# A Strassen-type output product, with two groups laced, for the last three tiles of a retention and bilinear-FFN kernel

## The chip, the cores and the metric

The kernel runs on one core of one Trainium2 chip. The metric is the device time of one launch in microseconds; the lower the better. Engines are named as in the profile: PE (TensorE, the matmuls), PEld (its weight loads), DVE (VectorE), ACT (ScalarE), POOL (GpSimd), SP (SyncE, which here only issues DMAs).

## The reference

Four batches of eight heads, 768 positions and head size 64 go through a recurrent retention, and its output, 3072 tokens of 512 values, through a bilinear feed-forward layer. All inputs and the output are float32.

```
gamma = 1.0 - 2.0 ** (-5.0 - arange(H))
for t in range(S):
    state = gamma * state + einsum('bhd,bhe->bhde', k[:, :, t], v[:, :, t])
    y[:, :, t] = scale * einsum('bhd,bhde->bhe', q[:, :, t], state)
x = y.transpose(0, 2, 1, 3).reshape(3072, 512)
a = x @ w_a          # 512 x 1536
b = x @ w_b          # 512 x 1536
out = (a * b) @ w_out  # 1536 x 512
```

## The kernel before

The tokens lie in 24 slots of 128. The feed-forward layer takes them in eight tiles `J` of 4, 2, 2, 2, 2, 4, 4 and 4 slots (`TILES`). The retention works in chunks of one slot: `casts(t)` scales k and q by powers of gamma on GpSimd, casts v, and has a DMA transpose k and q; `turn(new, old)` issues the scores of two new slots with their masks on VectorE (`scores`), the updates of the state, and the outputs of two old slots (`inter`, `intra`, `leave`), which become columns of the tile's `xt`. The first six slots go through `casts2`, `scores2` and their like, which work on pairs.

A block `ft` of the layer (`ffn_ab`, 12 blocks in a tile) computes 128 of the 1536 hidden values for all tokens of the tile: four matmuls into `a`, an ACT copy of it into `asb` (bf16), four matmuls into `g`, and on VectorE the product of `g` (in PSUM) and `asb` into `ht[J][:, ft]` (line 445). After the blocks, `ffn_out(J, i)` multiplies row `i` of the tile (128 tokens): 12 matmuls, one for each `ft`, with `ht` as weights and 512 columns of `wo_bf` streaming, accumulated in one PSUM bank `o`, copied by ACT into `osb` and stored. The last row of the last tile is cut into 256, 128 and 128 columns, the middle one copied by VectorE.

Every engine's order is the program's order: `seq` ties each instruction to the one before it on its engine. The order of the work is written out by hand at the end of the function: blocks, turns, casts and output rows of different tiles stand between one another, so that TensorE has work while others wait. What runs in tiles 5 to 7 before the change:

```
    blocks(5, 6, 9)
    turn(20, 18)
    blocks(5, 9, NFT)
    outs(5, 0, 1, 2, 3)
    blocks(6, 0, 4)
    turn(22, 20)
    blocks(6, 4, 9)
    turn(None, 22)
    blocks(6, 9, NFT)
    outs(6, 0, 1, 2, 3)
    blocks(7, 0, NFT)
    outs(7, 0, 1, 2, 3)
```

PSUM has eight banks: a ring of three for `a`, `g`, `o` and some scores (tag "ff"), one each for `y0` and `y1`, a pair for `at`, one for the state. Weights arrive in float32 slices in the pool `wstage` (four buffers each for two tags, 4 KB a partition), issued by SyncE in the order of `LOADS`, and are cast by GpSimd (`cast_w`, `cast_o`) into `wa_bf`, `wb_bf` and `wo_bf`. Each load waits for the cast that frees its buffer; the loads behind it in SyncE's queue wait with it. Stores of tiles 0 to 4 are held until the next block and issued by SyncE, those of tiles 5 to 7 by ACT.

Of the kernel before, what the change touches and what calls it, by code (L numbers as in the profile page):

```python
# [9 lines left out]
F32 = mybir.dt.float32  # L10
BF16 = mybir.dt.bfloat16
AF = mybir.ActivationFunctionType
ALU = mybir.AluOpType


TILES = [4, 2, 2, 2, 2, 4, 4, 4]
# [7 lines left out]
def kernel(  # L24
# [10 lines left out]
    nc = tc.nc  # L35
    P = 128
    B, H, S, D = q.shape
    NCH = S // P
    HP = H // 2
    DM = H * D  # L40
    DFF = moe_w_a.shape[1]
    KT = DM // P
    NFT = DFF // P
    NSLOT = B * NCH
    NW = 6
    WC = DFF // NW
    FPW = NFT // NW
    NO = 6
    FPO = NFT // NO
# [3 lines left out]

    const = ctx.enter_context(tc.tile_pool(name="const", bufs=1))
    wpool = ctx.enter_context(tc.tile_pool(name="wpool", bufs=1))
    wstage = ctx.enter_context(tc.tile_pool(name="wstage", bufs=4))
    raw = ctx.enter_context(tc.tile_pool(name="raw", bufs=3))
    nat = ctx.enter_context(tc.tile_pool(name="nat", bufs=6))
    tra = ctx.enter_context(tc.tile_pool(name="tra", bufs=4))
# [3 lines left out]
    osbp = ctx.enter_context(tc.tile_pool(name="osbp", bufs=6))  # L63
    psff = ctx.enter_context(tc.tile_pool(name="psff", bufs=3, space=bass.MemoryType.PSUM))
    psat = ctx.enter_context(tc.tile_pool(name="psat", bufs=1, space=bass.MemoryType.PSUM))
# [6 lines left out]
    def seq(bi):  # L72
        ins = bi.ins
        prev = last.get(ins.engine)
        if prev is not None:
            tc.add_manual_dep(ins, prev.name, nosync, reason="program order")
        last[ins.engine] = ins
        return bi


    raws, wst, whole = {}, {}, {}
# [17 lines left out]

    def load_w(j):  # L100
        for nm, src in (("a", moe_w_a), ("b", moe_w_b)):
            st = wstage.tile([P, KT, WC], F32, tag="w" + nm, name="wst" + nm)
            s = src[:, j * WC : (j + 1) * WC].rearrange("(c p) f -> p c f", p=P)
            seq(nc.sync.dma_start(out=st, in_=s))
            wst[nm, j] = st

    def load_o(j):
        st = wstage.tile([P, FPO, DM], F32, tag="w" + "ab"[j % 2], name="wsto")
        s = moe_w_out[j * FPO * P : (j + 1) * FPO * P, :].rearrange("(c p) d -> p c d", p=P)
        seq(nc.sync.dma_start(out=st, in_=s))  # L110
        wst["o", j] = st
# [3 lines left out]
    def issue_loads(n):  # L115
        for _ in range(min(n, len(pending))):
            what = pending.pop(0)
            {"p": load_pair, "s": load_slot, "w": load_w, "o": load_o}[what[0]](int(what[1:]))
# [2 lines left out]
    kqb = {}  # L121
    kqb = {}
    issue_loads(6)
    zero = const.tile([P, HP * P], F32, name="zero")
    seq(nc.vector.memset(zero, 0.0))  # L125
    lgr = const.tile([P, 1, H], F32, name="lgr")
    bq = const.tile([P, 1], F32, name="bq")
# [26 lines left out]
    for par in range(2):  # L154
        m = const.tile([P, 1, P], BF16, name=f"mask{par}")
# [17 lines left out]
    wa_bf = wpool.tile([P, KT, DFF], BF16, name="wa_bf")  # L173
    wb_bf = wpool.tile([P, KT, DFF], BF16, name="wb_bf")
    wo_bf = wpool.tile([P, NFT, DM], BF16, name="wo_bf")

    def cast(engine, dst, src):
        if engine is nc.scalar:
            seq(nc.scalar.copy(dst, src))  # L179
        else:  # L180
            seq(engine.tensor_copy(dst, src))  # L181
# [13 lines left out]
    first = 0  # L195
# [36 lines left out]
    def half(i):  # L232
        return slice(64 * i, 64 * i + 64)

    def scores(t, ff):
        if ff:
            at = [psff.tile([P, HP, P], F32, tag="ff", name=f"at{r}") for r in range(2)]
        else:
            both = psat.tile([P, 2, HP, P], F32, tag="at", name="at")
            at = [both[:, r] for r in range(2)]  # L240
        for hp in range(HP):
            for c in range(2):
                for r in range(2):
                    seq(nc.tensor.matmul(at[r][half(c), hp, :], kqT[t][half(r), 0, hp, half(c)],  # L244
                                         kqT[t][half(r), 1, hp, :], start=True, stop=True,
                                         skip_group_check=True))
        aT[t] = tra.tile([P, 2, HP, P], BF16, tag="aT", name="aT")
        for r in range(2):
            seq(nc.vector.tensor_tensor(aT[t][:, r], at[r], mask.to_broadcast([P, HP, P]), op=ALU.mult))  # L249
# [43 lines left out]
    def leave(t):  # L293
        J, i = where[t]
        if i == 0:
            xt[J] = xtp.tile([P, KT, 4 * P], BF16, tag="xt", name="xt")
        for r in range(2):
            seq(nc.scalar.copy(  # L298
                xt[J][:, 2 * r : 2 * r + 2, i * P : (i + 2) * P].rearrange(
                    "p j (s n) -> p j s n", s=2),  # L300
                ys[t // 2][r].rearrange("p (s j) n -> p j s n", s=2)))
# [23 lines left out]
    kqT2 = {}  # L325
# [19 lines left out]
    def scores2(u, par, ff=False):  # L345
        t = 2 * u + par
        if not ff:
            both = psat.tile([P, 2, HP, P], F32, tag="at", name="at")
            at = [both[:, r] for r in range(2)]
        else:  # L350
            at = [psff.tile([P, HP, P], F32, tag="ff", name=f"at{r}") for r in range(2)]
        for hp in range(HP):
            for c in range(2):
                for r in range(2):
                    seq(nc.tensor.matmul(at[r][half(c), hp, :],  # L355
                                         kqT2[u][half(r), par, 0, hp, half(c)],
                                         kqT2[u][half(r), :, 1, hp, half(c)],
                                         start=True, stop=True, skip_group_check=True))
        aT[t] = tra.tile([P, 2, HP, P], BF16, tag="aT", name="aT")
        for r in range(2):  # L360
            seq(nc.vector.tensor_tensor(aT[t][:, r], at[r], masks[par].to_broadcast([P, HP, P]),  # L361
                                        op=ALU.mult))
# [48 lines left out]
    def xcols(J, kt, c0, c1):  # L411
        if J < 2:
            return xt[J][:, c0 // P : c1 // P, kt, :]
        return xt[J][:, kt, c0:c1]
# [7 lines left out]
    ht = {}  # L422

    asbs = {}
# [13 lines left out]
    def ffn_g(J, ft, c0=0, c1=None):  # L438
        c1 = TILES[J] * P if c1 is None else c1
        fs = slice(ft * P, (ft + 1) * P)  # L440
        g = psff.tile([P, 4 * P], F32, tag="ff", name="g")[:, : c1 - c0]
        for kt in range(KT):
            seq(nc.tensor.matmul(g, wb_bf[:, kt, fs], xcols(J, kt, c0, c1),  # L443
                                 start=(kt == 0), stop=(kt == KT - 1)))
        seq(nc.vector.tensor_tensor(ht[J][:, ft, c0:c1], g, asbs.pop((J, ft, c0)), op=ALU.mult))  # L445

    def ffn_ab(J, ft):
        store()
        ffn_a(J, ft)
        ffn_g(J, ft)  # L450

    held = []

    def store():
        for dst, src in held:
            seq(nc.sync.dma_start(out=dst, in_=src))
        held.clear()

    def ffn_out(J, i):
        store()  # L460
        n0 = (sum(TILES[:J]) + i) * P
        osb = osbp.tile([P, DM], F32, tag="osb", name="osb")
        ends = J == len(TILES) - 1 and i == TILES[J] - 1
        cols = [(0, DM // 2), (DM // 2, 3 * DM // 4), (3 * DM // 4, DM)] if ends else [(0, DM)]
        for c0, c1 in cols:
            o = psff.tile([P, DM], F32, tag="ff", name="o")[:, : c1 - c0]
            for ft in range(NFT):
                seq(nc.tensor.matmul(o, ht[J][:, ft, i * P : (i + 1) * P], wo_bf[:, ft, c0:c1],  # L468
                                     start=(ft == 0), stop=(ft == NFT - 1)))
            cast(nc.vector if c0 == DM // 2 else nc.scalar, osb[:, c0:c1], o)  # L470
            if c0 == DM // 2:
                continue
            b0 = DM // 2 if c0 else 0
            dst, src = out[n0 : n0 + P, b0:c1], osb[:, b0:c1]
            if J < 5:
                held.append((dst, src))
            else:
                seq((nc.sync if c0 else nc.scalar).dma_start(out=dst, in_=src))

    D_, G_, A_ = nc.vector, nc.gpsimd, nc.scalar  # L480
    K, Q = 0, 1
# [5 lines left out]
    flip2(0, Q, [((0,), D_)])  # L487
    warm(psat, "y1", 256)
    scores2(0, 1)
    scores2(0, 0, True)  # L490
    update2(0, 0)
    warm(psat, "y1", 512)
# [60 lines left out]
    def blocks(J, a, b):  # L553
        for ft in range(a, b):
            ffn_ab(J, ft)

    def outs(J, *rows):
        for i in rows:
            ffn_out(J, i)

    casts(6)
    blocks(1, 0, 3)
    casts(7)
    blocks(1, 3, NFT)
    outs(0, 0, 1)
    casts(8)
    outs(0, 2, 3)
    casts(9)
# [42 lines left out]
    blocks(5, 6, 9)  # L611
    turn(20, 18)
    blocks(5, 9, NFT)
    outs(5, 0, 1, 2, 3)
    blocks(6, 0, 4)
    turn(22, 20)
    blocks(6, 4, 9)
    turn(None, 22)
    blocks(6, 9, NFT)
    outs(6, 0, 1, 2, 3)  # L620
    blocks(7, 0, NFT)
    outs(7, 0, 1, 2, 3)


# [28 lines left out]
```

## Time and profile before

| | |
|---|---|
| time, median of 3 runs | 231.83 us (231.5 to 232.21) |
| span of the profiled execution | 229.7 us, 5165 instructions |
| granted TensorE clock, mean | 0.998 |
| PE busy | 223.5 us (97%), 2108 matmuls |
| DVE, ACT, POOL busy | 95.1, 85.5, 77.0 us (41, 37, 34%) |
| output product, matmuls of 512 columns | 276 |
| HBM read, written | 28.31 MB, 6.29 MB |

The span runs from the first to the last instruction of one profiled execution; its own time as a launch is not given apart from the runs, whose times also contain what lies around the span. Times in the traces count from the span's start. In the groups of instructions the columns are: line, engine, operation, written tile <- read tiles, shapes, count, then busy microseconds and mean nanoseconds of one, then the engine's idle time before them and what ended it. In the chain the columns are start, microseconds, and what. In the timeline they are start, microseconds, engine, line and operation.

### The profile page before, as it was taken

To read this page: it belongs to the slowest core of one execution; us is meant where nothing else is said; L and a number is where in the kernel's file an instruction comes from. 1 tells how busy PE (TensorE), PEld (TensorE's weight loads), DVE (VectorE), ACT (ScalarE), POOL (GpSimd) and SP (SyncE) were. 2 spreads that over 40 slices of the span, in tenths; PEclk is the share of its full clock that TensorE was granted. 3 is DMA by queue.
4 is the path that set the end of the run, shared out by engine and by line. 5 is a ranking of instruction groups with operands and counts; after the bars stand their busy time and mean duration, and the time that the engine had idled before them with its cause. 6 is when DMAs were issued, how large, how long until landed. Compare 5 with 4: busy or idle time off the path is not lost.

```text
span 229.7 us, 5165 instructions
## 1 busy us (share of the span) xinstructions
PE 223.5 (97%) x2108; PEld 130.2 (57%) x2108; DVE 95.1 (41%) x178; ACT 85.5 (37%) x176; POOL 77.0 (34%) x98
## 2 busy tenths in 40 slices
PE   7899999999999999999999999999999999999994
PEld 3567445686456866887685454544454444444443
DVE  3785348542041565463644264620264310243300
ACT  3364334342225334454443453622343422433222
POOL 5355776776634254544633643200000000000000
PEclk9999999999999999999999999999999999999999
DMA  6999999999999999999999999402200002100022
GB/s 168 290 328 351 348 277 361 377 213 223 248 171 270 239 231 231 232 205 176 246 187 214 219 262 185 93 0 103 79 3 0 3 25 112 46 0 3 0 91 91
DMA packets 96118, 39.64 MB, mean 173 GB/s; under 512 B 76000, under 2 KB 91616, under 8 KB 96096
## 3 DMA queue, kind: packets, MB, share of 16 engines
q1 hardware_dynamic: 94368, 36.32, 73.8%
q10 hardware_dynamic: 1728, 3.02, 3.5%
q8 instruction: 16, 0.26, 0.5%
q14 instruction: 6, 0.05, 0.1%
HBM read 28.31 MB, written 6.29 MB: 151 GB/s over the span
## 4 chain that ended last, share of the span: by engine, by line
PE 94%; DMA 2%; DVE 2%; issue 0%; SPq 0%; ACT 0%; DVEq 0%
PE o L468 27%; PE g L443 27%; PE a L433 27%; DMA qf<-in_q_dram 2%; PE at L244 2%; PE y L289 2%; PE st L260 2%; PE y L398 1%; PE tp L342 1%; PE idle L419 1%; DVE kqb L213 1%; PE y L280 1%; PE st L375 1%; PE at L355 1%; PE y L387 1%; DVE aT L361 1%
## 5 line engine op out<-in xcount | busy, mean ns | idle before, releaser
L445 DVE TENSOR_TENSOR ht<-g,asb 128x256 bf16<-128x256 f32 (+1 forms) x98 | 53.9, 550 | 101.8 <-PE g L443 86.7
L433 PE MATMUL a<-xt,wa_bf 128*128 128x256 bf16 (+1 forms) x392 | 78.3, 323 | 0.0
L443 PE MATMUL g<-xt,wb_bf 128*128 128x256 bf16 (+1 forms) x392 | 77.8, 323 | 0.0
L436 ACT CAST asb<-a 128x256 bf16<-128x256 f32 (+1 forms) x98 | 46.2, 472 | 69.1 <-PE a L433 69.0
L468 PE MATMUL o<-wo_bf,ht 128*128 128x512 bf16 (+2 forms) x312 | 64.1, 363 | 0.0
L443 PEld LDWEIGHTS <-wb_bf 128*128 128x128 bf16 x392 | 38.2, 98 | 23.8
L433 PEld LDWEIGHTS <-wa_bf 128*128 128x128 bf16 x392 | 37.7, 98 | 24.0 <-issue 0.3
L468 PEld LDWEIGHTS <-ht 128*128 128x128 bf16 x312 | 29.0, 98 | 31.6
L213 POOL TENSOR_TENSOR kqb<-kf,ktab 128x512 bf16<-128x512 f32 x22 | 22.8, 1042 | 46.7 <-DMA kf<-in_k_dram 43.6
L179 ACT COPY osb<-o 128x512 f32<-128x512 f32 (+2 forms) x25 | 14.1, 564 | 50.3 <-PE o L468 38.3
L249 DVE TENSOR_TENSOR aT<-at,mask 128x512 bf16<-128x512 f32 x36 | 22.3, 683 | 1.4 <-PE at L244 1.1
L213 POOL TENSOR_TENSOR kqb<-qf,qtab 128x512 bf16<-128x512 f32 x18 | 18.8, 1042 | 2.2 <-DMA qf<-in_q_dram 1.3
L181 POOL CAST vb<-vf 128x512 bf16<-128x512 f32 x24 | 14.5, 610 | 9.3 <-DMA vf<-in_v_dram 8.4
L298 ACT CAST xt<-y 128x512 bf16<-128x512 f32 x18 | 9.7, 589 | 2.0 <-PE y L289 1.9
L419 PE MATMUL idle<-zero 128*128 128x256 f32 (+2 forms) x16 | 8.2, 631 | 1.6 <-DVE zero L125 1.5
L361 DVE TENSOR_TENSOR aT<-at,mask 128x512 bf16<-128x512 f32 x12 | 7.4, 683 | 1.2 <-PE at L355 1.2
L179 ACT CAST gst<-st 128x256 bf16<-128x256 f32 x13 | 4.8, 372 | 8.1 <-PE st L260 8.1
L181 POOL CAST wb_bf<-wstb 128x1024 bf16<-128x1024 f32 x6 | 6.2, 1040 | 4.1 <-DMA wstb<-in_moe_w_b_dram 4.1
L181 POOL CAST wa_bf<-wsta 128x1024 bf16<-128x1024 f32 x6 | 6.2, 1040 | 2.5 <-DMA wsta<-in_moe_w_a_dram 2.5
L181 POOL CAST wo_bf<-wsto 128x1024 bf16<-128x1024 f32 x6 | 6.2, 1040 | 2.3 <-DMA wsto<-in_moe_w_out_dram 2.3
L244 PE MATMUL at<-kqT 64*64 64x128 bf16 x288 | 5.9, 219 | 0.0
L380 ACT CAST gbd<-st 64x256 bf16<-64x256 f32 x10 | 3.7, 366 | 5.4 <-PE st L375 5.1
(45 smaller groups left out, 77.3 us busy)
## 6 DMA issues: line engine op xcount, KB each, us to landing
kf<-in_k_dram SPq DMA_DIRECT2D x18, 256.0 KB, 4.7
qf<-in_q_dram SPq DMA_DIRECT2D x18, 256.0 KB, 4.8
vf<-in_v_dram SPq DMA_DIRECT2D x18, 256.0 KB, 4.7
wsta<-in_moe_w_a_dram SPq DMA_DIRECT2D x6, 512.0 KB, 8.7
wstb<-in_moe_w_b_dram SPq DMA_DIRECT2D x6, 512.0 KB, 8.8
wsto<-in_moe_w_out_dram SPq DMA_DIRECT2D x6, 512.0 KB, 8.7
out_dram<-osb SPq DMA_DIRECT2D x12, 256.0 KB, 4.3
out_dram<-osb ACTq DMA_DIRECT2D x11, 256.0 KB, 2.0
```

What stands on the lines that cost most here:

```text
L179: seq(nc.scalar.copy(dst, src))
L181: seq(engine.tensor_copy(dst, src))
L213: seq(eng.tensor_tensor(dst, src, tab, op=ALU.mult))
L244: seq(nc.tensor.matmul(at[r][half(c), hp, :], kqT[t][half(r), 0, hp, half(c)], kqT[t][half(r), 1, hp, :], start=True, stop=True, skip_grou ...
L249: seq(nc.vector.tensor_tensor(aT[t][:, r], at[r], mask.to_broadcast([P, HP, P]), op=ALU.mult))
L298: seq(nc.scalar.copy(xt[J][:, 2 * r : 2 * r + 2, i * P : (i + 2) * P].rearrange("p j (s n) -> p j s n", s=2), ys[t // 2][r].rearrange("p ( ...
L419: seq(nc.tensor.matmul(idle[:, :n], zero[:, :P], zero[:, :n], start=True, stop=True, skip_group_check=True))
L433: seq(nc.tensor.matmul(a, wa_bf[:, kt, fs], xcols(J, kt, c0, c1), start=(kt == 0), stop=(kt == KT - 1)))
L436: seq(nc.scalar.copy(asb, a))
L443: seq(nc.tensor.matmul(g, wb_bf[:, kt, fs], xcols(J, kt, c0, c1), start=(kt == 0), stop=(kt == KT - 1)))
L445: seq(nc.vector.tensor_tensor(ht[J][:, ft, c0:c1], g, asbs.pop((J, ft, c0)), op=ALU.mult))
L468: seq(nc.tensor.matmul(o, ht[J][:, ft, i * P : (i + 1) * P], wo_bf[:, ft, c0:c1], start=(ft == 0), stop=(ft == NFT - 1)))
```

## The change

For tiles 5, 6 and 7 the output product is done with seven products of half-size blocks in place of eight (Strassen's scheme in Winograd's form). In the 2x2 blocking, the rows of the left matrix are even and odd tokens (`r`), the inner halves are `ft` 0 to 5 and 6 to 11 (`k2`), and the column halves are 256 of the 512 output values (`c`). A tile of 512 tokens makes two groups of 256. Each group takes seven products of six matmuls of 256 columns, `p1` to `p7`, in three PSUM banks A, B and C: bank A keeps accumulating p1, p6, p5 and p3, with a copy by ACT (`snap`) after each of the first three; B accumulates p7 and p4; C holds p2. VectorE adds the banks and the copies into the output rows. `double` writes the 14 products of both groups in one laced order.

The left sums S1 to S4 (`hsum`) are made on VectorE in twelve pieces a tile, spread over blocks 5 to 11 (`WHEN`). The right sums T1 to T4 (`weight_sums`) are made once, in two halves of four operations, after the first output row of tile 0. For tiles from 5 on, the product into `ht` puts even tokens ahead of odd ones in each group, and so reads `g` and `asb` with a step of two elements. For room, the staged weights go from eight buffers under two tags to six under one, which T1 and the left sums share later; the zero tile uses a buffer of the output rows; the pair `at` becomes two tags, and A and B of the two groups use the banks of y0, y1, at0 and at1, C the ring "ff". All stores of tiles 5 to 7 are issued by SyncE.

```
-    wstage = ctx.enter_context(tc.tile_pool(name="wstage", bufs=4))
+    wstage = ctx.enter_context(tc.tile_pool(name="wstage", bufs=6))
...
-            st = wstage.tile([P, KT, WC], F32, tag="w" + nm, name="wst" + nm)
+            st = wstage.tile([P, KT, WC], F32, tag="w", name="wst" + nm)
...
-        st = wstage.tile([P, FPO, DM], F32, tag="w" + "ab"[j % 2], name="wsto")
+        st = wstage.tile([P, FPO, DM], F32, tag="w", name="wsto")
...
-    zero = const.tile([P, HP * P], F32, name="zero")
+    zero = osbp.tile([P, DM], F32, tag="osb", name="zero")
...
-            both = psat.tile([P, 2, HP, P], F32, tag="at", name="at")
-            at = [both[:, r] for r in range(2)]
+            at = [psat.tile([P, HP, P], F32, tag=f"at{r}", name="at") for r in range(2)]
...
-        seq(nc.vector.tensor_tensor(ht[J][:, ft, c0:c1], g, asbs.pop((J, ft, c0)), op=ALU.mult))
+        dst, x, y = ht[J][:, ft, c0:c1], g, asbs.pop((J, ft, c0))
+        if J >= SCHEME:
+            dst = dst.rearrange("p (u r n) -> p u r n", r=2, n=P)
+            x, y = (z.rearrange("p (u n r) -> p u r n", r=2, n=P) for z in (x, y))
+        seq(nc.vector.tensor_tensor(dst, x, y, op=ALU.mult))
...
+    def weight_sums(a, b):
+        if not T1:
+            T1.append(wstage.tile([P, NP, DH], BF16, tag="w", name="wsum1"))
+        j = slice(a, b)
+        tt(T3[:, j], B22[:, j], B12[:, j], ALU.subtract)
+        tt(T2[:, j], T3[:, j], B11[:, j], ALU.add)
+        tt(T4[:, j], B21[:, j], T2[:, j], ALU.subtract)
+        tt(T1[0][:, j], B12[:, j], B11[:, j], ALU.subtract)
...
+    def hsum(J, s, a, b):
+        U = TILES[J] // 2
+        if (J, s) not in hs:
+            hs[J, s] = wstage.tile([P, NP, 2, P], BF16, tag="w", name=f"hs{s}")
+        v = ht[J].rearrange("p (k j) (u r n) -> p r k j u n", k=2, r=2, n=P)
+        A11, A12, A21, A22 = (v[:, r, k2, a:b, :U] for r in range(2) for k2 in range(2))
+        S = {x: hs[J, x][:, a:b, :U] for x in (1, 2, 3, 4) if (J, x) in hs}
+        x, y, op = {3: (A11, A21, ALU.subtract), 2: (A22, S[3], ALU.subtract), 1: (A21, A22, ALU.add),
+                    4: (A12, S.get(2), ALU.subtract)}[s]
+        tt(S[s], x, y, op)
+
+    WHEN = {5: ["302"], 6: ["324"], 7: ["346", "202"], 8: ["102", "402"], 9: ["224", "124"],
+            10: ["424"], 11: ["246", "146", "446"]}
...
+        def product(self, bank, left, right, first):
+            if first:
+                pool, tag = self.tags[bank]
+                self.bank[bank] = pool.tile([P, 4 * P], F32, tag=tag, name="m" + bank)[:, :DH]
+            m, J = self.bank[bank], self.J
+            for j in range(NP):
+                if isinstance(left, int):
+                    w = hs[J, left][:, j, self.i]
+                else:
+                    r, k2 = left
+                    i = 2 * self.i + r
+                    w = ht[J][:, NP * k2 + j, i * P : (i + 1) * P]
+                seq(nc.tensor.matmul(m, w, right[:, j], start=(first and j == 0), stop=(j == NP - 1),
+                                     skip_group_check=True))
...
+        def snap(self, n):
+            if n == 0:
+                self.snaps = tra.tile([P, 3, DH], F32, tag="kqT2", name="snaps", bufs=2)
+            seq(nc.scalar.copy(self.snaps[:, n], self.bank["A"]))
...
+        def p1(self):
+            self.product("A", (0, 0), B11, True)
+            self.snap(0)
+
+        def p2(self):
+            self.product("C", (0, 1), B21, True)
+            tt(self.row(0)[:, :DH], self.bank["C"], self.snaps[:, 0], ALU.add)
+
+        def p6(self):
+            self.product("A", 2, T2, False)
+            self.snap(1)
+
+        def p7(self):
+            self.product("B", 3, T3, True)
+
+        def p5(self):
+            self.product("A", 1, T1[0], False)
+            self.snap(2)
+            tt(self.row(1)[:, DH:], self.bank["B"], self.snaps[:, 2], ALU.add)
+            if self.J == len(TILES) - 1:
+                self.leave(1, DH, DM)
+
+        def p3(self):
+            self.product("A", 4, B22, False)
+            seq(nc.scalar.copy(self.row(0)[:, DH:], self.bank["A"]))
+            self.leave(0)
+
+        def p4(self):
+            self.product("B", (1, 1), T4, False)
+            tt(self.row(1)[:, :DH], self.bank["B"], self.snaps[:, 1], ALU.add)
+            self.leave(1, 0, DH if self.J == len(TILES) - 1 else DM)
...
+    def double(J):
+        a, b = Group(J, 0, Y0, AT0, FF), Group(J, 1, Y1, AT1, FF)
+        for g, p in ((a, "p1"), (a, "p7"), (b, "p1"), (b, "p7"), (a, "p6"), (a, "p2"), (b, "p6"),
+                     (a, "p5"), (b, "p2"), (b, "p5"), (a, "p3"), (a, "p4"), (b, "p3"), (b, "p4")):
+            getattr(g, p)()
...
             ffn_ab(J, ft)
+            if J >= SCHEME:
+                sums(J, ft)
...
-    outs(0, 0, 1)
+    outs(0, 0)
+    weight_sums(0, 3)
+    weight_sums(3, 6)
+    outs(0, 1)
...
-    outs(5, 0, 1, 2, 3)
+    double(5)
...
-    outs(6, 0, 1, 2, 3)
+    double(6)
     blocks(7, 0, NFT)
-    outs(7, 0, 1, 2, 3)
+    double(7)
```

More of the change, by code (lines that the diff above doesn't have):

```diff
@@ L175 @@
     wo_bf = wpool.tile([P, NFT, DM], BF16, name="wo_bf")
+    NP = NFT // 2
+    DH = DM // 2
+    wsum = wpool.tile([P, 3, NP, DH], BF16, name="wsum")
+    wo_v = wo_bf.rearrange("p (two j) (c d) -> p two c j d", two=2, c=2)
+    B11, B12, B21, B22 = (wo_v[:, k2, c] for k2 in range(2) for c in range(2))
+    T2, T3, T4 = (wsum[:, n] for n in range(3))
+    SCHEME = 5
     def cast(engine, dst, src):
@@ L347, in scores2 @@
         if not ff:
-            both = psat.tile([P, 2, HP, P], F32, tag="at", name="at")
-            at = [both[:, r] for r in range(2)]
+            at = [psat.tile([P, HP, P], F32, tag=f"at{r}", name="at") for r in range(2)]
         else:
@@ L478, in ffn_out, with tt @@
                 seq((nc.sync if c0 else nc.scalar).dma_start(out=dst, in_=src))
+    def tt(dst, x, y, op):
+        seq(nc.vector.tensor_tensor(dst, x, y, op=op))
+    T1 = []
+    def weight_sums(a, b):
[6 more added lines that the diff above has]
+        tt(T1[0][:, j], B12[:, j], B11[:, j], ALU.subtract)
@@ new lines @@
+    hs = {}
+    def hsum(J, s, a, b):
[8 more added lines that the diff above has]
+        tt(S[s], x, y, op)
@@ new lines, with sums, __init__, row @@
+    WHEN = {5: ["302"], 6: ["324"], 7: ["346", "202"], 8: ["102", "402"], 9: ["224", "124"],
+            10: ["424"], 11: ["246", "146", "446"]}
+    def sums(J, ft):
+        for what in WHEN.get(ft, []):
+            hsum(J, *map(int, what))
+    class Group:
+        def __init__(self, J, i, A, B, C):
+            self.J, self.i, self.tags = J, i, {"A": A, "B": B, "C": C}
+            self.bank = {}
+            self.osb = {}
+        def product(self, bank, left, right, first):
[16 more added lines that the diff above has]
+            seq(nc.scalar.copy(self.snaps[:, n], self.bank["A"]))
+        def row(self, r):
+            if r not in self.osb:
+                self.osb[r] = osbp.tile([P, DM], F32, tag="osb", name="osb")
+            return self.osb[r]
+        def leave(self, r, c0=0, c1=DM):
+            n0 = (sum(TILES[: self.J]) + 2 * self.i) * P
+            dst = out[n0 : n0 + 2 * P, :].rearrange("(n r) d -> r n d", r=2)[r, :, c0:c1]
+            if self.J < 5:
+                held.append((dst, self.osb[r][:, c0:c1]))
+            else:
+                seq(nc.sync.dma_start(out=dst, in_=self.osb[r][:, c0:c1]))
+        def p1(self):
[23 more added lines that the diff above has]
+            self.leave(1, 0, DH if self.J == len(TILES) - 1 else DM)
@@ L480 @@
+    FF = (psff, "ff")
+    Y0, Y1, AT0, AT1 = ((psat, x) for x in ("y0", "y1", "at0", "at1"))
+    def double(J):
[3 more added lines that the diff above has]
+            getattr(g, p)()
     D_, G_, A_ = nc.vector, nc.gpsimd, nc.scalar
```

## The prediction

> **What bounds the kernel now.** I read the page first (shares, chain by line), then the chain in order of time, then the groups kept apart by shape, then the timeline around the places that the change touches.
>
> ```profile
> core 0: 229.7 us, clock 0.998
> PE 223.5 (97%) x2108; PEld 130.2 (57%) x2108; DVE 95.1 (41%) x178; ACT 85.5 (37%) x176; POOL 77.0 (34%) x98
> PE 94%; DMA 2%; DVE 2%; issue 0%; SPq 0%; ACT 0%; DVEq 0%
> ```
>
> The chain that ended last is 94% TensorE at a granted clock of 0.998. "Busy" alone would not say that (matmuls are pipelined); the chain does: TensorE releases itself nearly all the time, so the time is the number of columns that it streams, and other engines matter only where they make it wait. The chain in order of time gives the price of a column:
>
> ```profile
> 72.00 0.44 PE a L433 x4
> ...
> 82.04 0.44 PE g L443 x4
> 82.48 0.24 PE st L260 x8
> ...
> 151.34 10.36 PE o L468 x48
> 185.03 10.36 PE o L468 x48
> ...
> 216.11 10.43 PE o L468 x72
> ```
>
> From 72.00 to 82.48 lie the twelve blocks of tile 2: 12 x (4 + 4) = 96 matmuls of 256 columns in 10.48 us, 109.2 ns each, without a break. The output products of tiles 5 and 6 are 48 matmuls of 512 columns in 10.36 us, 215.8 ns each, so half a matmul costs 1.2% over half the price. Tile 7 has 36 of 512, 12 of 256 and 24 of 128 columns (its last row is cut in three): 36 x 215.8 + 12 x 109.2 = 9.08 us, which leaves 1.35 us for the 24 small ones, 56 ns each.
>
> **What is removed on TensorE.** A tile of four rows of 128 tokens now takes 2 groups x 7 products x 6 matmuls of 256 columns = 84, instead of 48 of 512. 84 x 109.2 ns = 9.17 us. Tiles 5 and 6 win 10.36 - 9.17 = 1.19 us each, tile 7 wins 10.43 - 9.17 = 1.26 us: **3.64 us** in all. The 36 additional weight loads per tile have to hide:
>
> ```profile
> L443 PEld LDWEIGHTS <-wb_bf 128*128 128x128 bf16 x392 | 38.2, 98 | 23.8
> L445 DVE TENSOR_TENSOR ht<-g,asb 128x512 bf16<-128x512 f32 x46 | 31.8, 692 | 68.8 <-PE g L443 68.8
> L445 DVE TENSOR_TENSOR ht<-g,asb 128x256 bf16<-128x256 f32 x52 | 22.1, 425 | 33.0 <-PE g L443 17.8 <-ACT asb L436 15.1
> L213 DVE TENSOR_TENSOR kqb<-kf,ktab 128x512 bf16<-128x512 f32 x2 | 1.3, 688 | 0.9 <-DMA kf<-in_k_dram 0.9
> L181 DVE COPY kqT<-tp 128x512 bf16<-128x512 bf16 x4 | 1.7, 423 | 0.2 <-PE tp L342 0.2
> L181 DVE COPY kqT<-tp 128x1024 bf16<-128x1024 bf16 x1 | 0.7, 691 | 0.7 <-PE tp L342 0.7
> L181 DVE CAST xt<-y 128x512 bf16<-128x512 f32 x2 | 1.5, 739 | 1.8 <-PE y L398 1.8
> L179 ACT COPY osb<-o 128x256 f32<-128x256 f32 x1 | 0.4, 372 | 0.7 <-PE o L468 0.7
> L179 ACT COPY osb<-o 128x128 f32<-128x128 f32 x1 | 0.3, 265 | 1.0 <-PE o L468 1.0
> ```
>
> A weight load shows 98 ns, under the 109.2 ns of a 256-column matmul, and the small matmuls of tile 7 ran at 56 ns with such loads between them, so loads do not set the pace. I count them at nothing.
>
> **Waits between products.** Each product reuses a PSUM bank after an ACT copy (bank A: copy, then p6, copy, p5, copy, p3) or after a VectorE addition (bank B: p5's sum, then p4). A product lasts 6 x 109.2 = 0.66 us. In the laced order, at least two other products lie between the end of a use of bank A and its next use: 1.31 us, against an ACT copy of 256 columns of 0.37 us. Bank B's next use comes three products (1.97 us) after p5 in group a and in group b: one copy of 0.37 and one addition of about 0.43 (the 256-column row with a PSUM operand, 425 ns). All of it fits with half a microsecond or more to spare; without the lacing each of the 8 reuses per tile would show. ACT's four copies a group take 8 x 0.37 = 3.0 us of 9.17. Nothing is charged. The A, B and C banks are those of y, at and ff, which nothing else uses during the product; splitting the pair "at" into two tags adds no bank.
>
> **The sums on VectorE.** New: 12 pieces a tile (512 elements each, bf16 from and to SBUF) after blocks 5 to 11, one, one, two, two, two, one, three; and the 36 products into ht of tiles 5 to 7 now read PSUM and asb with a step of two elements. No row shows a tensor-tensor operation with all operands bf16 in SBUF. Its bounds: 423 ns (a bf16 copy of 512 elements, 0.52 ns for each further element by the 1024 row) and 688 ns (the tensor-tensor of 512 from f32). I take 423, because the slope of the copy shows that this engine handles two bf16 elements in the time of one f32. [...] For the product with a step of two, the lower bound is 692 ns; a cast that writes with a step of two took 739, which I take; the upper bound is twice the slope of the 256 and 512 rows (267 ns for 256 elements): 692 + 533 = 1225 ns. A block lasts 2 x 0.86 = 1.73 us on TensorE; VectorE's need in a block with two pieces is 0.74 + 2 x 0.42 = 1.59 us. So it keeps up, narrowly. After block 11 three pieces take 1.27 us after the product into ht; p6 of group a, the first to need them, comes 4 x 0.66 = 2.62 us after the start. Nothing.
>
> The tight place is tile 5, where the scores of a turn lie between blocks 8 and 9:
>
> ```profile
> 142.81 0.69 DVE L445 TENSOR_TENSOR ht<-g,asb 128x512 bf16<-128x512 f32 x1 [1.03 <-PE g L443]
> 144.54 0.69 DVE L445 TENSOR_TENSOR ht<-g,asb 128x512 bf16<-128x512 f32 x1 [1.04 <-PE g L443]
> 145.15 2.47 DVE L249 TENSOR_TENSOR aT<-at,mask 128x512 bf16<-128x512 f32 x4
> 147.99 0.69 DVE L445 TENSOR_TENSOR ht<-g,asb 128x512 bf16<-128x512 f32 x1 [0.37 <-PE g L443]
> 147.02 0.86 PE g L443 x4
> 147.88 0.86 PE a L433 x4
> ```
>
> VectorE had 0.37 us to spare before block 9's product. The four masks now stand behind two sums of block 8. Two of the masks free the ff banks that g of block 9 (147.02) and a of block 10 (147.88) write. With 0.42 a piece: 144.54 + 0.74 + 0.85 = 146.13, first mask done at 146.75, second at 147.37: both just in time; block 9's product is 0.6 us late, which blocks 10 and 11 absorb. With 0.69 a piece: block 7's pieces end at 144.88, block 8's at 146.95, first mask at 147.57, **0.55 us** late for g. I charge 0.1 us here. Tile 6 has its turn with scores before block 4, ahead of any sum.
>
> **Weight sums.** Eight operations of 768 elements, 0.56 us each by the copy rows (0.423 + 0.134) or at most 0.96 (0.688 + 0.267): 4.5 to 7.7 us, queued on VectorE after the last product of tile 1.
>
> ```profile
> 54.38 0.42 DVE L445 TENSOR_TENSOR ht<-g,asb 128x256 bf16<-128x256 f32 x1 [0.45 <-PE g L443]
> 64.92 0.42 DVE L181 CAST gst<-st 128x256 bf16<-128x256 f32 x1 [10.12 <-PE st L260]
> ```
>
> VectorE idles there for 10.12 us: free at either end of the bound.
>
> **Six staging buffers for eight.** Weight slices 3a to 5b now wait for the cast of a slice three before, not four, and all loads behind them on SyncE wait too.
>
> ```profile
> 15.58 1.04 POOL L181 CAST wa_bf<-wsta 128x1024 bf16<-128x1024 f32 x1 [0.34 <-DMA wsta<-in_moe_w_a_dram]
> 15.78 2.82 SPq L104 DMA_DIRECT2D wsta<-in_moe_w_a_dram  x1
> 18.48 1.04 POOL L181 CAST wb_bf<-wstb 128x1024 bf16<-128x1024 f32 x1 [1.86 <-DMA wstb<-in_moe_w_b_dram]
> 18.65 1.42 SPq L104 DMA_DIRECT2D wstb<-in_moe_w_b_dram  x1
> 37.11 1.04 POOL L181 CAST wa_bf<-wsta 128x1024 bf16<-128x1024 f32 x1 [0.31 <-DMA wsta<-in_moe_w_a_dram]
> 38.45 1.02 PE a L433 x4
> wsta<-in_moe_w_a_dram SPq DMA_DIRECT2D x6, 512.0 KB, 8.7
> ```
>
> Slice 3a goes out at 16.6 (its cast ends) instead of 15.8, 3b at 19.5 instead of 18.65: some 0.9 us later. A load takes 8.7 us to land, and the issues themselves last 1.4 to 2.8 us, so transfers are queued; the queue gets shorter and does not run dry. I take nothing or little (0.1 us). The bound on the other side is the whole delay, 0.9 us, for a of block 10 in tile 0 starts 0.3 us after its weights' cast ends (37.11 + 1.04 = 38.15, then 38.45). No gain can come from fewer buffers.
>
> **The end and the stores.**
>
> ```profile
> 226.57 0.27 ACT L179 COPY osb<-o 128x128 f32<-128x128 f32 x1 [0.97 <-PE o L468]
> 226.86 0.36 SPq L478 DMA_DIRECT2D out_dram<-osb  x1
> 140.55 5.11 SPq L226 DMA_TRANSPOSE kqT<-kqb  x2
> out_dram<-osb SPq DMA_DIRECT2D x1, 128.0 KB, 1.7
> ```
>
> After the last matmul stood an ACT copy of 128 columns (0.27) and a 128 KB store; now a VectorE addition of 256 columns (0.43) and a store of the same size: +0.16 us. A 256 KB store starts about 0.4 us ahead of it on the same queue; I add 0.1 us, at most 0.5. Moving the other stores from ACT's queue to SyncE's costs nothing: SyncE's loads are all issued by 145.7. The zero tile's new place is free long before the first output row.
>
> **The sum.** 3.64 - 0.16 - 0.1 (end) - 0.1 (turn) - 0.1 (loads) = 3.2 us: the span goes from 229.7 to about 226.5. The runs' median of 231.83 us lies 2.1 us above the profiled span (the runs go from 231.5 to 232.21), which I leave as it is: **228.6 us**. The case's own ends: 3.64 - 0.16 with 0.3 for the spread of runs gives 227.8; a gain of 2.6 gives 229.2.
>
> **Rivals.**
>
> *Stepped reads are slow.* If the product into ht takes the upper bound, 1.225 us, blocks with two pieces need 2.07 us against 1.73. Tile 7 falls behind by 0.35 three times; the ring of three ff banks allows 1.73 - 0.1 - 1.23 = 0.4 us, so 0.65 us shows. Tile 6 recovers in the turn between blocks 8 and 9 and loses nothing. Tile 5 loses 0.6 at g of block 9 and 0.5 at a of block 11. Sum 1.75: 230.35 us. [...] Against the rival stand the 739 ns of the stepped write, though that is a write to SBUF.
>
> *The sums run one element at a time* (0.69): tile 5 loses 0.55 and some 0.25 after it, tile 7 about 0.1: 229.5 us.
>
> *The loads fall behind by their whole 0.9 us*: 229.4 us.
>
> *VectorE becomes the bound* (slower). If both bounds hold, blocks 7 to 9 need 1.225 + 1.38 = 2.6 us against 1.73 and the one-piece blocks 1.91: 3 x 0.88 + 3 x 0.19 = 3.2 us behind, less 0.4: 2.8 us in tile 7, about 1.9 in tile 6 (a turn's 0.9 us helps), about 3.6 in tile 5 (the masks): 8.3 us, **236.9 us**. It decides from about 2.25 us of VectorE work in a two-piece block, where the stalls eat 3.2 us. For it speaks that no row shows either operation; against it the two-element copy and the stepped write.
>
> *The columns are saved and come back as waits between products* (the change does not do what it says): 0.13 us at each of the 24 reuses of a bank would take back 3.2 us, for 231.8 us; the 1.31 us of cover speak against it.
>
> **How the numbers follow.** Forecast 0.62; stepped reads 0.11; slow sums 0.08; late loads 0.08; VectorE bound 0.06; waits between products 0.05. The range 227.8 to 230.5 takes in the first four and leaves the last two out. A measurement of this kernel tells about 0.3% (0.7 us) from no change. The first four are faster by more than that, less 0.02 for ends that reach no change: 0.87; no change 0.05; slower 0.08.
>
> **What would show it.** In the new trace: the output product of tiles 5, 6 and 7 as 84 matmuls in 9.2 us each without gaps; sums at 0.42 us; the product into ht of tiles 5 to 7 near 0.69 to 0.74; the idle time before TensorE in blocks 7 to 11 of tiles 5 and 7 near nothing; a of block 10 in tile 0 still near 38.45. Wrong if the sums or the stepped products take over 0.7 and 1.0 us, if gaps open between products, or if tile 1 starts later than before.

## The result and the profile after

| kernel | median, us | runs, us | against before (95% interval) |
|---|---|---|---|
| before | 231.67 | 231.43 to 232.21 | |
| after | 229.12 | 228.71 to 229.73 | 0.9892 (0.9871 to 0.9912) |
| after, second measurement | 229.02 | 228.43 to 229.34 | 0.9881 (0.9866 to 0.9897), before at 231.69 |

The change makes the kernel faster by 2.55 us, 1.1%; 228.6 was forecast. The profiled span went from 229.7 to 227.5 us. First the page of the changed kernel, its shares of busy time and the chain's engines:

```profile
span 227.5 us, 5402 instructions
PE 218.4 (96%) x2177; PEld 139.1 (61%) x2192; DVE 121.8 (54%) x239; ACT 87.3 (38%) x187; POOL 78.4 (34%) x98
PE 86%; DMA 6%; DVE 3%; SPq 2%; issue 1%; POOL 0%; DVEq 0%
```

The change adds 84 matmuls, each with a weight load, to the 2108 of before: the 2192 loads are there, and 15 matmul records are missing from the trace. TensorE's share of the chain fell from 94% to 86%: the chain now goes through something else for a while. In the names, `hs` are the left sums, `wsum` the right sums, `aT` the masked scores, `mA` to `mC` the banks A to C. The chain in order of time says where:

```profile
127.17 0.86 PE a L438 x4
...
140.40 4.45 DMA qf<-in_q_dram
145.27 1.98 DVE hs L490 x2
147.25 0.61 DVE aT L255
147.90 1.02 PE g L448 x4
...
152.38 0.66 PE mA L542 x6
...
160.89 0.66 PE mB L542 x6
...
184.88 0.66 PE mA L542 x6
...
214.77 0.66 PE mA L542 x6
...
223.29 0.67 PE mB L542 x6
```

Set against the times of before this gives the whole account. Tile 5 starts 0.12 us late (127.17 for 127.05). g of block 9 in tile 5 starts at 147.90 for 147.02, and the output product of tile 5 at 152.38 for 151.34: 0.92 us more are lost in between. That product ends at 160.89 + 0.66 = 161.55, 9.17 us later, as tile 6's does in its place. Tile 7's starts at 214.77 for 216.11 and ends at 223.96 for 226.54. From there to the end of the span it takes 3.54 us for 3.16. So: -1.19 - 1.19 - 1.24 + 0.12 + 0.92 + 0.38 = -2.2 us of span. What lies outside the span also fell, from 1.8 to 2.05 us in the runs of before whose spans are on record to 1.7 (229.16 us for the profiled run). Every version with the scheme shows 1.65 to 1.8; why stays open.

The sums are in one view: the instructions of line 490, with minimum, median and maximum duration in nanoseconds.

```profile
L490 DVE TENSOR_TENSOR hs<-ht x18: 414/415/1207, 140.1 to 216.0; 128x512 bf16<-128x512 bf16 x18
L490 DVE TENSOR_TENSOR hs<-ht,hs x18: 415/418/850, 143.9 to 216.3; 128x512 bf16<-128x512 bf16 x18
L490 DVE TENSOR_TENSOR wsum<-wo_bf x4: 550/590/1392, 54.8 to 59.6; 128x768 bf16<-128x768 bf16 x4
L454 DVE TENSOR_TENSOR ht<-g,asb 128x512 bf16<-128x512 f32 x46 | 31.8, 690 | 39.3 <-PE g L448 39.3
```

The medians are 415 and 418 ns, close to the 423 of the forecast; the maxima are 1207 and 850 ns, three and two times that. The last line (from the groups by shape) shows the product into ht at 690 ns, with the steps of tiles 5 to 7, where it was 692 without. What the long sums have beside them, the timeline of tile 5 shows (the brackets give the engine's idle time before the instruction and what ended it):

```profile
143.91 1.28 POOL L220 TENSOR_TENSOR kqb<-kf,ktab 128x512 bf16<-128x512 f32 x1 [2.41 <-DMA kf<-in_k_dram]
144.66 0.69 DVE L454 TENSOR_TENSOR ht<-g,asb 128x512 bf16<-128x512 f32 x1 [0.37 <-PE g L448]
145.15 1.04 POOL L220 TENSOR_TENSOR kqb<-qf,qtab 128x512 bf16<-128x512 f32 x1
145.27 1.21 DVE L490 TENSOR_TENSOR hs<-ht 128x512 bf16<-128x512 bf16 x1
...
146.36 0.61 POOL L188 CAST vb<-vf 128x512 bf16<-128x512 f32 x1 [0.17 <-DMA vf<-in_v_dram]
146.40 0.85 DVE L490 TENSOR_TENSOR hs<-ht,hs 128x512 bf16<-128x512 bf16 x1
147.17 2.47 DVE L255 TENSOR_TENSOR aT<-at,mask 128x512 bf16<-128x512 f32 x4
147.90 1.02 PE L448 MATMUL g<-xt,wb_bf 128*128 128x512 bf16 x4 [0.76 <-DVE aT L255]
```

The first long sum starts inside GpSimd's second multiplication for slot 23, the second inside its cast. Neither merely runs slower. GpSimd's multiplication ends at 146.19 and the sum at 146.48; the cast ends at 146.97 and the sum at 147.25. In all the profiles of this case a sum of 512 elements that starts inside a GpSimd operation, with 0.19 us or more of that left, ends 0.27 to 0.29 us after it, be it a multiplication or a cast. The other way round it is alike: the multiplication at 143.91 starts just behind a sum of 0.42 us and takes 1.28 us for 1.04. So the one that comes second is held up by the first: the sum by 0.80 us where 0.92 us of the multiplication were left, the multiplication by 0.24 where 0.38 of the sum were left. The masks start 1.0 us later than the forecast's working had it (147.17 for 146.13), and g of block 9, which needs the bank that the first mask frees, waits 0.76 us. Those four matmuls then take 1.02 us of the chain for 0.86, which makes up the 0.92 us. The product into ht at 144.66, which reads one operand from PSUM, keeps its 0.69 us inside the multiplication that runs from 143.91 to 145.19.

### The profile page after: what moved, and what is told of

Read it like the earlier page. It is cut to its first block, busy times and chain, and to the rows that moved or that the text cites. A ratio compares the mean times of both kernels' runs of the same rounds, so it can differ in the third digit from the quotient of the medians.

```text
span 227.5 us, 5402 instructions
## 1 busy us (share of the span) xinstructions
PE 218.4 (96%) x2177; PEld 139.1 (61%) x2192; DVE 121.8 (54%) x239; ACT 87.3 (38%) x187; POOL 78.4 (34%) x98
## 4 chain that ended last, share of the span: by engine, by line
PE 86%; DMA 6%; DVE 3%; SPq 2%; issue 1%; POOL 0%; DVEq 0%
PE g L448 25%; PE a L438 25%; PE o L477 14%; PE mA L542 7%; DMA qf<-in_q_dram 4%; PE mB L542 3%; DMA kf<-in_k_dram 2%; PE at L250 2%; PE mC L542 2%; PE y L295 1%; PE st L266 1%; PE y L403 1%; SPq L233 1%; PE tp L348 1%; PE idle L424 1%; DVE hs L490 1%
## 5 line engine op out<-in xcount | busy, mean ns | idle before, releaser
L477 PE MATMUL o<-wo_bf,ht 128*128 128x512 bf16 x137 | 32.1, 380 | 0.4
L255 DVE TENSOR_TENSOR aT<-at,mask 128x512 bf16<-128x512 f32 x36 | 22.3, 681 | 1.5 <-PE at L250 1.2
L477 PEld LDWEIGHTS <-ht 128*128 128x128 bf16 x144 | 13.5, 98 | 15.7
L186 ACT COPY osb<-o 128x512 f32<-128x512 f32 x12 | 7.0, 585 | 24.0 <-PE o L477 24.0
L542 PEld LDWEIGHTS <-hs 128*128 128x128 bf16 x144 | 14.1, 98 | 1.6
L548 ACT COPY snaps<-mA 128x256 f32<-128x256 f32 x18 | 6.7, 372 | 14.9 <-PE mA L542 14.9
L542 PEld LDWEIGHTS <-ht 128*128 128x128 bf16 x108 | 10.6, 98 | 1.9
L490 DVE TENSOR_TENSOR osb<-mB,snaps 128x256 f32<-128x256 f32 x12 | 5.1, 424 | 9.4 <-ACT snaps L548 5.3
L542 PE MATMUL mA<-wsum,hs 128*128 128x256 bf16 x72 | 9.3, 273 | 0.0
L490 DVE TENSOR_TENSOR hs<-ht 128x512 bf16<-128x512 bf16 x18 | 8.3, 459 | 0.0
L490 DVE TENSOR_TENSOR hs<-ht,hs 128x512 bf16<-128x512 bf16 x18 | 8.0, 444 | 0.2
```

Of the source, the lines that this page charges most:

```text
L490: seq(nc.vector.tensor_tensor(dst, x, y, op=op))
L542: seq(nc.tensor.matmul(m, w, right[:, j], start=(first and j == 0), stop=(j == NP - 1), skip_group_check=True))
```

## Experiments

Theory A: VectorE's sums of two SBUF operands and GpSimd's work slow one another; in tile 5 that makes masks and products late, and TensorE waits for the banks. Rivals: VectorE is over-full there anyway (B); the pause comes from later loads or casts, not from the sums; or it is an accident of one execution. The first four kernels below were measured beside before at 231.69 us, the last four beside before at 231.61 us; the ratios are to that.

**The changed kernel again.** No edit.

> The changed kernel once more, unaltered, as the base for the kernels beside it on the same chip. Both theories: 2.2 to 2.9 us under the kernel before, the 84 matmuls of each output product in 9.17 us, and a pause of 0.5 to 0.9 us in front of g of block 9 in tile 5. If that pause is an accident of one execution (a third theory), it is missing here.

229.02 us, span 227.6. The pause is there but in another place. From the timeline:

```profile
143.65 1.04 POOL L220 TENSOR_TENSOR kqb<-kf,ktab 128x512 bf16<-128x512 f32 x1 [2.47 <-DMA kf<-in_k_dram]
143.69 1.28 DVE L490 TENSOR_TENSOR hs<-ht 128x512 bf16<-128x512 bf16 x1
144.82 1.05 POOL L220 TENSOR_TENSOR kqb<-qf,qtab 128x512 bf16<-128x512 f32 x1
144.90 1.26 DVE L490 TENSOR_TENSOR hs<-ht,hs 128x512 bf16<-128x512 bf16 x1
146.08 0.68 DVE L454 TENSOR_TENSOR ht<-g,asb 128x512 bf16<-128x512 f32 x1
...
146.81 1.02 PE L438 MATMUL a<-xt,wa_bf 128*128 128x512 bf16 x4 [0.48 <-DVE ht L454]
148.08 1.02 PE L448 MATMUL g<-xt,wb_bf 128*128 128x512 bf16 x4 [0.25 <-DVE aT L255]
```

GpSimd's work came a quarter of a microsecond earlier and met the sums of block 7 instead of block 8: block 8's product into ht is 1.3 us late, a of block 9 waits 0.48 us for it, g of block 9 0.25 us more. The same loss, by another instruction. GpSimd's multiplication of k starts when a DMA lands (at 143.91 us in the first profile, at 143.65 in this one), so the meeting is not fixed. The eight runs of the changed kernel spread over 1.3 us (228.43 to 229.73), the 24 of before over 0.8 (231.39 to 232.21). That the meeting makes the spread is borne out by the versions below: the four in which sums and multiplications do not meet in tile 5 spread over 0.10 to 0.40 us, the other three, like each of the two measurements of the changed kernel, over 0.7 to 1.0.

**Sums of block 8 behind the masks.**

```
-            if J >= SCHEME:
+            if J >= SCHEME and (J, ft) != (5, 8):
                 sums(J, ft)
...
     turn(20, 18)
+    sums(5, 8)
```

> The two sums of block 8 in tile 5 are issued behind the four masks of the turn instead of ahead of them. Theory A (the sums lie in front of the masks on VectorE and are stretched to 1.98 us by GpSimd's multiplications): the pause in front of g of block 9 goes from 0.76 to under 0.1 us, and the time falls by 0.7 to 0.9 us against the changed kernel. Theory B (VectorE is over-full in this stretch whatever the order): the pause only moves to block 10 or 11 and the time falls by under 0.3 us.

228.70 us, 0.9868 (0.9853 to 0.9883): 0.3 us less, not 0.7 to 0.9, and the intervals overlap. Theory A's expectation missed here, because it had taken block 8 for the place. GpSimd's work met the sums of block 7 again, which were not moved:

```profile
143.62 1.21 DVE L490 TENSOR_TENSOR hs<-ht 128x512 bf16<-128x512 bf16 x1
144.75 1.26 DVE L490 TENSOR_TENSOR hs<-ht,hs 128x512 bf16<-128x512 bf16 x1
145.93 0.68 DVE L454 TENSOR_TENSOR ht<-g,asb 128x512 bf16<-128x512 f32 x1
146.53 2.47 DVE L255 TENSOR_TENSOR aT<-at,mask 128x512 bf16<-128x512 f32 x4
146.66 1.02 PE L438 MATMUL a<-xt,wa_bf 128*128 128x512 bf16 x4 [0.41 <-DVE ht L454]
```

Taken alone, this run speaks as much for B: the pause moved to a of block 9 (0.41 us), and a of block 11 was late too. It does not tell the two apart.

**GpSimd without the multiplications of slot 23.**

```
-        scaled(nc.gpsimd, t, 0)
-        scaled(nc.gpsimd, t, 1)
+        if t == NSLOT - 1:
+            seq(nc.gpsimd.memset(kqb[t], 0.0))
+        else:
+            scaled(nc.gpsimd, t, 0)
+            scaled(nc.gpsimd, t, 1)
```

> The sums stay ahead of the masks. GpSimd does not multiply k and q of the last slot by the tables; it fills that tile with zeros instead (this leaves out the scores of the last slot). Theory A: with no GpSimd multiplication beside them the two sums of block 8 take 0.41 to 0.42 us each instead of 1.21 and 0.85, the first mask ends about 0.05 us before g needs its bank, and the time falls by 0.7 to 0.9 us. Theory B' (two sums ahead of the masks are too much even undisturbed): the pause stays at 0.3 us or more and the time falls by under 0.5 us.

228.22 us, 0.9850 (0.9835 to 0.9864), without the scores of the last slot. The sums stand where they stood:

```profile
145.33 0.51 DVE L493 TENSOR_TENSOR hs<-ht 128x512 bf16<-128x512 bf16 x1
145.76 0.41 DVE L493 TENSOR_TENSOR hs<-ht,hs 128x512 bf16<-128x512 bf16 x1
146.09 2.47 DVE L258 TENSOR_TENSOR aT<-at,mask 128x512 bf16<-128x512 f32 x4
```

Block 7's take 0.41 and 0.42 us, block 8's 0.51 (it starts inside the one cast left to GpSimd, 0.23 us before that ends) and 0.41; the masks start at 146.09 and g of block 9 at 147.21 without a pause. That speaks against B: undisturbed, two sums ahead of the masks fit.

**The scheme from tile 6 on.**

```
-    SCHEME = 5
+    SCHEME = 6
...
-    double(5)
+    outs(5, 0, 1, 2, 3)
```

> Tile 5 goes back to the plain output product and has no sums; tiles 6 and 7 keep the scheme. Theory A: tile 5 gained 1.19 us by its product and lost 0.8 to 0.9 by the pause, so the time rises by only 0.2 to 0.5 us against the changed kernel, and g of block 9 starts without a pause. If the pause has nothing to do with the sums (loads, casts or transposes that came later), it stays, and the time rises by about 1.2 us.

229.37 us, 0.9897 (0.9881 to 0.9914). Taking tile 5's saving of 1.19 us away costs 0.35 us against 229.02, a difference within the overlapping intervals of the two, and far from 1.2. Without sums, g of block 9 starts unpaused at 147.10, although GpSimd's multiplications run even later (144.55 and 145.72) than in the changed kernel. Later loads and casts alone do not make the pause.

**GpSimd's slot 23 held until the sums are done.**

```
-    casts(23)
...
     blocks(5, 9, NFT)
+    gate = const.tile([P, 1], BF16, name="gate")
+    seq(nc.gpsimd.tensor_copy(gate, hs[5, 4][:, NP - 1, 1, P - 1 :]))
+    casts(23)
```

> All work is kept. GpSimd's work for slot 23 is held until the last sum of tile 5 is written (it first copies one column of that sum). Theory A (sums and GpSimd's multiplications slow one another, and tile 5's masks and products are late by it): sums of blocks 7 and 8 at 0.41 to 0.42 us each, no pause before block 9 or 10, the time 0.7 to 0.9 us under the changed kernel's 229.0, that is 228.1 to 228.3. If leaving out the multiplications helped only by the missing loads or scores, the time stays within 0.3 us of 229.0.

228.11 us (227.97 to 228.37), 0.9851 (0.9838 to 0.9865), all work kept. This is the fastest version measured and beats both kernels.

```profile
145.40 0.41 DVE L490 TENSOR_TENSOR hs<-ht 128x512 bf16<-128x512 bf16 x1
145.73 0.42 DVE L490 TENSOR_TENSOR hs<-ht,hs 128x512 bf16<-128x512 bf16 x1
146.07 2.48 DVE L255 TENSOR_TENSOR aT<-at,mask 128x512 bf16<-128x512 f32 x4
...
153.59 0.19 POOL L743 COPY gate<-hs 128x1 bf16<-128x1 bf16 x1 [14.50 <-PE mA L542]
153.73 1.04 POOL L220 TENSOR_TENSOR kqb<-kf,ktab 128x512 bf16<-128x512 f32 x1
```

Every sum of tile 5 takes 0.41 to 0.43 us, and the masks start at 146.07. The prediction's working, with the lower price of a sum, had 146.13. Theory A is shown: removing the overlap, by leaving GpSimd's work out or by moving it, takes 0.8 to 0.9 us off.

**Row stores of tile 7 on ACT's queue.**

```
-                seq(nc.sync.dma_start(out=dst, in_=self.osb[r][:, c0:c1]))
+                q = nc.scalar if self.J == 7 and r == 0 else nc.sync
+                seq(q.dma_start(out=dst, in_=self.osb[r][:, c0:c1]))
```

> The two 256 KB stores of whole rows in tile 7 go out on ACT's queue, so that the last store on SyncE's queue has no large one right ahead of it. If the queue is what makes the end 0.38 us longer than before (3.54 us from the last matmul to the end, 3.16 before), the end falls to about 3.3 us, of which 0.16 is VectorE's longer last addition, and the time by 0.2 us. If the end is longer only by that addition and by the store itself, nothing moves by over 0.1 us.

228.55 us, 0.9865 (0.9851 to 0.9878), but not by the end. TensorE finished at 223.52 in a span of 227.0: 3.48 us, against 3.54 and 3.46 in the two profiles of the changed kernel, whose spans are given to 0.1 us. What was smaller in this profile was tile 5's pause (0.38 us), which moves from run to run. The next kernel has that pause removed.

**Both edits.**

> Both edits together. If they are independent: the sum of the two, 228.0 us or a little less.

228.25 us, 0.9857 (0.9842 to 0.9872): not the 228.0 expected, 0.14 us over the version with only GpSimd's work moved, and no better. Its end takes 3.50 us, that version's 3.43. The queue is not what makes the end longer. VectorE's last addition accounts for 0.15 us (0.42 for 0.27); what makes the remaining 0.1 to 0.2 us was not settled.

**The two groups one after the other.**

```
-        for g, p in ((a, "p1"), (a, "p7"), (b, "p1"), (b, "p7"), (a, "p6"), (a, "p2"), (b, "p6"),
-                     (a, "p5"), (b, "p2"), (b, "p5"), (a, "p3"), (a, "p4"), (b, "p3"), (b, "p4")):
+        for g, p in [(g, p) for g in (a, b) for p in ("p1", "p7", "p6", "p2", "p5", "p3", "p4")]:
```

> The same 14 products, one group wholly ahead of the other (p1 p7 p6 p2 p5 p3 p4). By the prediction's account, p3 then follows p5 in bank A at once and waits for ACT's copy: 0.37 us and some 0.08 around it, in each of six groups, 2.7 us in all; p6 and p4 keep one product or more of cover and do not wait. The time rises from 229.0 to about 231.7. If the waits are paid elsewhere already, or a copy of the bank does not hold the next product up, it stays near 229.

232.26 us, 1.0030 (1.0020 to 1.0041): slower than the kernel before. From the chain, group a in tile 5:

```profile
154.59 0.67 PE mA L542 x6
155.26 0.02 issue
155.29 0.38 ACT snaps L548
155.67 0.04 issue
155.71 0.81 PE mA L542 x6
156.53 0.66 PE mB L542 x6
```

p3 waits for ACT's copy as expected, and nothing else in the group waits. The wait is 0.44 us long, but the six matmuls behind it also take 0.81 us of the chain for 0.66: each wait costs 0.60 us, 3.6 in six groups (3.2 by the medians of the runs, 2.7 expected). The timeline shows where the 0.15 us come from:

```profile
154.43 0.82 PE L542 MATMUL mA<-wsum,hs 128*128 128x256 bf16 x6
155.71 0.81 PE L542 MATMUL mA<-wo_bf,hs 128*128 128x256 bf16 x6 [0.46 <-ACT snaps L548]
156.36 0.82 PE L542 MATMUL mB<-wsum,ht 128*128 128x256 bf16 x6
```

The matmuls are no slower. A product takes 0.82 us from its first start to its last end wherever it stands, but one that does not wait starts 0.66 us after the one before it, so that the two overlap by some 0.16 us. A wait takes this overlap away. The lacing is worth the change's whole gain.

## Why the prediction was right, and where it was off

The sign, the range and the main term hold. The products cost what the 256-column row of tile 2 said: 9.17, 9.17 and 9.19 us for 9.17, hence 3.62 for 3.64 us. No wait between products shows in the laced order (0.66 us a product in the chain), and the lacing experiment shows that the cover which the prediction counted is real. It also shows that without the lacing two of the eight reuses in a tile wait, not each of them: the other six still have a product or more between. The stepped product into ht, which reads PSUM with a step of two f32, costs nothing (690 ns for 692; 739 was taken), so that rival is out. The sums run at the lower bound, 415 ns for 423. Their slope is the copy's too: a weight sum of 768 elements took 557 ns with GpSimd idle (at 56.30), 142 for the 256 more, where the copy rows gave 134 and the product into ht takes 267 for its 256 more. The staging buffers cost 0.03 us (a of block 10 in tile 0 at 38.48 for 38.45) where 0.1 was charged and 0.9 was the bound; what makes up the rest of the 0.12 us by which tile 5 starts late stays open.

The term that was mis-sized is tile 5's turn: 0.1 us charged, 0.92 measured. Its working was right for an undisturbed VectorE (the masks at 146.13 in the working, at 146.07 where GpSimd is held back), and the step that failed is the price of a sum: both bounds, 0.42 and 0.69, came from rows that GpSimd did not hold up (copies with their one input in PSUM, 0.42 us also for the one at 8.69 inside GpSimd's casts from 8.68 to 9.85, and two multiplications at 5.10 with GpSimd idle), and beside it a sum took up to 1.28 us. The prediction looked for what is queued behind the sums, not for what runs beside them. The trace of before had it in the same stretch:

```profile
142.18 1.04 POOL L213 TENSOR_TENSOR kqb<-kf,ktab 128x512 bf16<-128x512 f32 x1 [3.46 <-DMA kf<-in_k_dram]
143.35 1.04 POOL L213 TENSOR_TENSOR kqb<-qf,qtab 128x512 bf16<-128x512 f32 x1
144.55 0.61 POOL L181 CAST vb<-vf 128x512 bf16<-128x512 f32 x1 [0.16 <-PE g L443]
```

It even has a case of the delay: of VectorE's own multiplications of two SBUF operands, at 688 ns in the median, the one at 12.26 took 904 ns, and a GpSimd multiplication ran until 12.61.

The new trace has both cases: a sum with its two operands in SBUF went from 415 ns to 1207 inside one multiplication of slot 23, while the product into ht, with one operand in PSUM, kept 0.69 us inside the other.

The weight sums were hidden, as said, but not at the price: the eight took from 54.75 to 61.01, single ones up to 1.39 us for a bound of 0.96, and GpSimd's multiplications for slot 8 took 1.29 and 1.35 us for 1.04. The end cost 0.38 us, where 0.26 was charged. Without the collision the gain is 231.61 - 228.11 = 3.5 us, a little over the 3.2 forecast. That the runs of the changed kernel gained 2.55 us, where the spans of the two profiles differ by 2.2, is owed to what lies outside the span; the prediction left that as it was, so this part of its closeness is luck.

## What to carry to other kernels

When work is put into an engine's idle time, price it beside what the other engines run at that moment, and look in the trace for every operation for which it may have to wait: the length of an operation alone is a lower bound only (a sum here took 0.41 us alone and up to 1.28 beside GpSimd). Where two operations took turns here, the one that came second was late by most of what was left of the first: 0.80 us with 0.92 left, 0.43 with 0.57 left. An order that hides PSUM reuse can be worth all that a scheme saves (229.02 us with the lacing, 232.26 without, 231.61 before), and a wait can cost more than its length (0.60 us for 0.44). If a kernel's runs begin to spread, look for two streams whose meeting depends on when a DMA lands (here 0.7 to 1.0 us of spread with the meeting, 0.10 to 0.40 without).

## What the runs showed of the hardware

VectorE additions and subtractions of two bf16 SBUF tiles (512 elements) took 0.41 to 0.43 us alone. One that started inside a GpSimd multiplication or cast with 0.19 us or more of that left ended 0.27 to 0.29 us after it, so that it took up to 1.28 us; a cast counted like a multiplication, by what was left of it (0.51 us where 0.23 was left, 0.85 where 0.57 was). A GpSimd multiplication that started inside such a sum with 0.15 us or more of it left ended some 0.9 us after it, and so took up to 1.28 us for 1.04; beside the longer weight sums 1.29 and 1.35 us in the first profile. A product of g in PSUM and asb in SBUF kept its 0.69 us beside GpSimd. A wait of 0.44 us in front of six matmuls of 256 columns cost 0.60 us, because these no longer overlapped the six before them by 0.16 us.
